# Order of work in a two-layer kernel: attention front, PV sums, norms and kernel spectrum rearranged

## The chip, the cores and the metric

One NeuronCore of a Trainium2 chip runs the whole program. The metric is the device time of one execution in microseconds (us); three executions of the kernel before are given, and one more was profiled. TensorE is called PE, VectorE DVE, ScalarE ACT, GpSimd POOL and SyncE SP, as in the profile.

## The reference, cut to what matters

Four residual steps on x of 2048 positions by 512 channels: attention A, convolution B, A, B, with the same weights both times.

```python
def _A_ref(x, wqkv, wo):          # 32 heads of 16; each position sees 8 positions, 2 apart
    off = jnp.arange(8) * 2
    idx = pos[:, None] - off[None, :]
    ...
    logits = einsum("bhsd,bhswd->bhsw", q, kg) * scale
    logits = where(idx >= 0, logits, -1e9)
    o = einsum("bhsw,bhswd->bhsd", softmax(logits), vg)
    return o.reshape(B, S, D) @ wo

def _B_ref(u, A_re, ..., log_dt, Dskip):
    P = exp(logdA[:, :, None] * l)                # l = 0 .. 2047
    K = einsum("dn,dnl,dn->dl", Cc, P, dB).real   # a kernel of 2048 taps per channel
    y = irfft(rfft(pad(u)) * rfft(pad(K)))[:L]
    return y + u * Dskip

x = A_x
x = x + _A_ref(_layernorm(x), ...)
x = x + _B_ref(_layernorm(x), ...)
x = x + _A_ref(_layernorm(x), ...)
x = x + _B_ref(_layernorm(x), ...)
```

K depends on no x, so its spectrum is made once and used by both B layers.

## The kernel before, in words

Position s = 16 p + a lies on partition p in row a, so `x_sb` is [128, 16, 512] in f32. The source is plain Python that unrolls; a scheduler below it orders each engine's instructions by readiness and source order, and places all semaphores. Pools that are closed hand their memory to pools opened later.

1. `k_gen` makes K: 12 squarings give powers of the state matrix (setup), then four chunks of 32 channel groups build tables `A_r`, `A_i` on DVE (`cmul`, lines 618 to 633), multiply them with `B_r`, `B_n` on PE (line 760) and copy the result to `kgs` on ACT (line 764). Between the chunks `build_b_consts` is stepped: it makes the transform matrices, the large one going to DRAM (`w2_dram`, line 406). At the end 24 transfers write `kgs` to DRAM (line 780).
2. `k_spectrum` reads K back in another order (`k_load`, lines 787 and 803), permutes it to `k_perm` (line 585) and runs the two forward transform steps on it: `f1` (line 486) and `f2` (line 496), in two groups of channels g. The spectrum goes to `kf_dram` (line 599).
3. x is loaded, copied to f32 (line 863), and row sums and sums of squares are taken on ACT (lines 89 and 90).
4. `layer_a`, its front: `ln_finish` makes 1/std of all 16 rows with one power on POOL (line 112), `ln_apply` normalizes, PE transposes to `xnT` (line 148), and k is projected to `kT_ext` (lines 155 to 161). Fourteen rows stand ahead of `kT_ext`, shifted by one partition (lines 164 and 165).
5. `layer_a`, its core, in four quarters q of four rows: q projection (`qproj`); `prod` multiplies q with shifted k on DVE (line 204, 8 a quarter) and PE sums over a head's channels into L (line 207); softmax (lines 213 to 242); `pav` multiplies the weights with shifted v on DVE (line 255, 8 a quarter, one for each shift w and all four rows); PE adds these products up in `po` with the product as the loaded weights and the identity as the moving operand, which also transposes (line 259); `out_proj` (line 275) and the residual (line 95). Products of quarter q + 1 stand between the `pav` of quarter q. The weight for v and the output weight are loaded by `load_a_weights` ahead of the layer.
6. `b_layer`: the norm of all rows to `u`, then `f1`, `f2`; the product with the spectrum read from DRAM in four transfers a tile (lines 527, 528, 531, 532); back with `i1` (lines 543, 544) and `i2` (lines 556, 557) and the residual. `zip_run` runs two steps side by side, always one group's step beside the other's.
7. Layers 4 to 6 again; the last residuals are copied to bf16 on ACT and stored (lines 879, 880).

Of the kernel before, what the change touches and what calls it, by code (L numbers as in the profile page):

```python
# [10 lines left out]
ACT = mybir.ActivationFunctionType  # L11
# [22 lines left out]
POOL_PRODS = ()  # L34
POOL_PAVS = ()
# [7 lines left out]
def build_a_consts(tc, nc, cpool, tpool):  # L43
# [5 lines left out]
    c["ident"] = ident  # L49
# [9 lines left out]
    rows = cpool.tile([1, 2, 512], BF16, name="rows")  # L59
    nc.vector.memset(rows[:], 0.0)  # L60
    nc.vector.memset(rows[:, 0, 0:1], 1.0)
    c["e0"] = rows[:, 0, 0:P]
    c["zrow"] = rows[:, 1, :]
# [8 lines left out]
def load_a_weights(tc, nc, wpool, tmp, A_wqkv, A_wo):  # L72
    wqk = wpool.tile([P, NDT, 2 * D], BF16, name="wqk")
    wsrc = A_wqkv.rearrange("(dt p) c -> p dt c", p=P)
    nc.sync.dma_start(wqk[:], wsrc[:, :, 0:2 * D])
    wvraw = tmp.tile([P, NDT, D], BF16, name="wvraw")
    nc.sync.dma_start(wvraw[:], wsrc[:, :, 2 * D:3 * D])
    wv = wpool.tile([P, NDT, DH, H], BF16, name="wvp")
    nc.scalar.copy(wv[:], wvraw[:].rearrange("p t (h d) -> p t d h", h=H))
    wo = wpool.tile([P, NDT, D], BF16, name="wop")  # L80
    wo_v = A_wo.rearrange("(h q r) c -> r h q c", h=H, q=4, r=4)
    for r in range(4):
        nc.sync.dma_start(wo[r * 32:(r + 1) * 32, :, :], wo_v[r])
    return wqk, wv, wo


def ln_stats_part(nc, lnst, x_sb, a0, a1):
    for a in range(a0, a1):
        nc.scalar.activation(lnst["junk"][:], x_sb[:, a, :], ACT.Identity, accum_out=lnst["s1"][:, a, 0:1])
        nc.scalar.activation(lnst["junk"][:], x_sb[:, a, :], ACT.Square, accum_out=lnst["s2"][:, a:a + 1])  # L90
    nc.vector.memset(lnst["s1"][:, a0:a1, 1:2], 0.0)


def residual_add(nc, lnst, x_row, y_psum, a, part=0):
    nc.vector.scalar_tensor_tensor(x_row, y_psum, 1.0, x_row, ALU.mult, ALU.add, accum_out=lnst["s1"][:, a, part:part + 1])  # L95


def row_sumsq(nc, lnst, x_sb, a):
    nc.scalar.activation(lnst["junk"][:], x_sb[:, a, :], ACT.Square, accum_out=lnst["s2"][:, a:a + 1])  # L99


def ln_finish(nc, pool, lnst):
    mean = pool.tile([P, NA], F32, name="ln_mean")
    nc.vector.tensor_tensor(mean[:], lnst["s1"][:, :, 0], lnst["s1"][:, :, 1], ALU.add)
    nc.vector.tensor_scalar(mean[:], mean[:], 1.0 / D, None, ALU.mult)
    msq = pool.tile([P, NA], F32, name="ln_msq")
    nc.vector.tensor_tensor(msq[:], mean[:], mean[:], ALU.mult)
    veps = pool.tile([P, NA], F32, name="ln_veps")
    nc.vector.scalar_tensor_tensor(veps[:], lnst["s2"][:], 1.0 / D, msq[:], ALU.mult, ALU.subtract)
    nc.vector.tensor_scalar(veps[:], veps[:], EPS, None, ALU.add)  # L110
    rstd = pool.tile([P, NA], F32, name="ln_rstd")
    nc.gpsimd.tensor_tensor(rstd[:], veps[:], lnst["mh"][:], ALU.pow)
    nb = pool.tile([P, NA], F32, name="ln_nb")
    nc.vector.scalar_tensor_tensor(nb[:], mean[:], -1.0, rstd[:], ALU.mult, ALU.mult)
    return rstd, nb
# [9 lines left out]
def layer_a(tc, nc, x_sb, consts, wqk, wv, wo, lnst):  # L125
    ident, ind8 = consts["ident"], consts["ind8"]
    e0, zrow, maskrow = consts["e0"], consts["zrow"], consts["maskrow"]
    scale = float(DH) ** -0.5
    with ExitStack() as ctx:
        big = ctx.enter_context(tc.tile_pool(name="a_big", bufs=1))  # L130
        kT = big.tile([P, NDT, NA + 14, P], BF16, name="kT_ext")
        v = big.tile([P, NA + 14, D], BF16, name="v_ext")
        xnT = big.tile([P, NDT, NA * P], BF16, name="xnT")
        with ExitStack() as c1:
            p1 = c1.enter_context(tc.tile_pool(name="a_p1", bufs=1))
            ps_tr = c1.enter_context(tc.tile_pool(name="a_ps_tr", bufs=2, space=PSUM))
            ps_pj = c1.enter_context(tc.tile_pool(name="a_ps_pj", bufs=4, space=PSUM))
            rstd, nb = ln_finish(nc, p1, lnst)
            nc.vector.memset(lnst["s1"][:, :, 1:2], 0.0)
            xn = p1.tile([P, NA, D], BF16, name="xn")  # L140
            for a in range(NA):
                ln_apply(nc, xn[:, a, :], x_sb[:, a, :], rstd, nb, a, "act" if a % 3 != 2 else "dve")
            for ag in range(2):
                for dt in range(NDT):
                    pt = ps_tr.tile([P, 8, P], BF16, name="pt")
                    for j in range(8):
                        a = ag * 8 + j
                        nc.tensor.transpose(pt[:, j, :], xn[:, a, dt * P:(dt + 1) * P], ident[:])  # L148
                    nc.vector.tensor_copy(xnT[:, dt, ag * 8 * P:(ag + 1) * 8 * P], pt[:].rearrange("p j q -> p (j q)"))
# [17 lines left out]
        with ExitStack() as c2:  # L167
# [134 lines left out]
            for q in range(4):  # L302
# [3 lines left out]
                if n1 is not None:  # L306
                    prod(n1, 0); prod(n1, 1)
# [604 lines left out]
```

## Time and profile before

| | us |
|---|---|
| median of three runs | 721.57 |
| lowest, highest | 715.87, 723.58 |
| the profiled execution | 717.98 |
| its span, first to last instruction | 715.9 |
| busy PE, weight load | 381.7, 286.6 |
| busy DVE | 504.4 |
| busy ACT | 351.0 |
| busy POOL | 13.8 |

The mean granted TensorE clock was 0.802 of full speed. Two kinds of views are used below. In the page's slices the span is cut in 40 parts of 17.9 us, one digit each, the busy share in tenths. In the groups by line a row reads: line, engine, operation, output and inputs, shapes, count; then busy us and mean ns of one; then the idle time of the engine just before them and what ended it. In the views in order of time the first two numbers are start and length in us.

### The profile page before, as it was taken

The page shows a single profiled execution, that of the slowest core. Times are in us where ns is not written, and L with a number is a line of the kernel's source. Part 1 is how long each engine was busy: PE and PEld are TensorE (multiplying, and loading weights), DVE is VectorE, ACT ScalarE, POOL GpSimd, SP SyncE. Part 2 cuts the span into 40 slices and gives each one's busy share as a digit, 9 for nine tenths or more (in the row PEclk, how much of TensorE's full clock was granted, in tenths as well). Part 3 has the DMA queues.
Part 4 walks back from the last instruction along what each step waited for, and adds up shares of the span by engine and source line. Part 5 has one row for each costly group of instructions (what it writes and reads, how often), then busy time and mean ns, then how long its engine had stood idle before and what let it go on. Part 6 is the DMA issues. An engine that isn't in the chain of part 4 may idle for free. (4 is left out here: it accounts for less than half of the span.)

```text
span 715.9 us, 12534 instructions
## 1 busy us (share of the span) xinstructions
PE 381.7 (53%) x5166; PEld 286.6 (40%) x5192; DVE 504.4 (70%) x873; ACT 351.0 (49%) x552; POOL 13.8 (2%) x19
## 2 busy tenths in 40 slices
PE   1000222205500499989675744817998886746763
PEld 1000222205400244567454644714446576526652
DVE  7999999304500348899995867635689999858665
ACT  7998831106479644322332754285432531357524
POOL 0000000000000100000001000010000000010000
PEclk9999955556855599988788778767998987979787
DMA  2002110237661000300002766040003000083622
GB/s 52 0 29 88 60 59 1 73 85 233 214 220 38 0 1 2 103 2 1 2 1 100 234 195 181 1 118 1 1 23 82 2 1 2 2 320 116 195 76 118
DMA packets 28134, 54.28 MB, mean 76 GB/s; under 512 B 9347, under 2 KB 13344, under 8 KB 26144
## 3 DMA queue, kind: packets, MB, share of 16 engines
q1 hardware_dynamic: 25774, 50.87, 22.6%
q10 hardware_dynamic: 2304, 2.62, 1.0%
q8 instruction: 40, 0.66, 0.4%
q14 instruction: 16, 0.13, 0.1%
HBM read 38.67 MB, written 11.14 MB: 70 GB/s over the span
## 5 line engine op out<-in xcount | busy, mean ns | idle before, releaser
L259 PE MATMUL po<-ident,pav 128*128 128x128 bf16 x1024 | 77.4, 250 | 9.0 <-DVE pav L255 8.9
L259 PEld LDWEIGHTS <-pav 128*128 128x128 bf16 x1024 | 74.4, 115 | 11.6 <-DVE pav L255 11.4
L255 DVE TENSOR_TENSOR pav<-attn,v_ext 128x2048 bf16<-128x2048 bf16 x64 | 74.7, 1219 | 4.0 <-PE po L259 3.9
L204 DVE TENSOR_TENSOR prod<-qT,kT_ext 128x2048 bf16<-128x2048 bf16 x64 | 75.0, 1214 | 1.6 <-ACT qT L183 1.6
L760 PE MATMUL pk<-B_r,A_r 128*128 128x84 bf16 x128 | 16.5, 251 | 95.6 <-DVE A_r L629 95.6
L543 PE MATMUL pb<-Wp,t 128*128 128x128 bf16 x256 | 37.4, 240 | 32.6 <-DVE t L531 29.3
L760 PEld LDWEIGHTS <-A_r 128*128 128x128 bf16 x128 | 15.0, 130 | 96.2 <-ACT w_qi L398 66.8
L148 PE MATMUL pt<-ident,xn 128*128 128x128 bf16 x128 | 15.8, 278 | 69.4 <-ACT xn L120 67.2
L266 ACT CAST oT<-po 128x1024 bf16<-128x1024 f32 x8 | 8.1, 1012 | 87.3 <-PE po L259 87.3
L530 ACT CAST ub<-pb 128x1024 bf16<-128x1024 f32 x32 | 32.2, 1030 | 21.0 <-DVE t L532 19.7
L148 PEld LDWEIGHTS <-xn 128*128 128x128 bf16 x128 | 11.3, 124 | 74.6 <-ACT xn L120 71.2
L207 PE MATMUL L<-ind,prod 128*128 128x8 bf16 x1024 | 33.8, 167 | 13.2 <-DVE prod L204 13.1
L207 PEld LDWEIGHTS <-prod 128*128 128x128 bf16 x1024 | 31.2, 97 | 23.8 <-DVE prod L204 16.3
L543 PEld LDWEIGHTS <-t 128*128 128x128 bf16 x256 | 27.6, 109 | 30.1 <-DVE t L531 29.9
L99 ACT ACTIVATE ln_junk<-x_sb 128x512 bf16<-128x512 f32 x48 | 30.2, 629 | 15.2 <-DVE x_sb L95 13.9
L544 PE MATMUL pb<-WpJ,t 128*128 128x128 bf16 x256 | 36.0, 240 | 0.3 <-DVE t L532 0.3
L496 PE MATMUL pb<-a1s,w_sb 128*128 128x64 bf16 x768 | 31.0, 197 | 9.0 <-DVE kf_sb L475 3.3
L285 PE MATMUL pq<-wvp,xnT 128*128 128x512 bf16 x122 | 32.0, 391 | 2.0 <-DVE v_ext L290 1.5
L486 PE MATMUL pb<-F1c,u 128*64 128x128 bf16 x256 | 21.0, 251 | 21.6 <-issue 21.3
L275 PE MATMUL pq<-wop,oT 128*128 128x512 bf16 x120 | 28.9, 379 | 6.7 <-ACT oT L266 6.1
L473 ACT CAST z<-pb 128x1024 bf16<-128x1024 f32 x16 | 16.2, 1012 | 32.7 <-PE pb L544 32.5
L496 PEld LDWEIGHTS <-w_sb 128*128 128x128 bf16 x768 | 27.4, 100 | 12.1 <-issue 9.2
(205 smaller groups left out, 998.7 us busy)
## 6 DMA issues: line engine op xcount, KB each, us to landing
w_sb<-w_dram SPq DMA_DIRECT2D x12, 1024.0 KB, 7.7
kr_c<-kf_dram SPq DMA_DIRECT2D x64, 128.0 KB, 2.9
ki_c<-kf_dram SPq DMA_DIRECT2D x64, 128.0 KB, 2.9
kf_dram<-kf_sb SPq DMA_DIRECT2D x16, 256.0 KB, 2.6
v_ext<-v_ext SPq DMA_DIRECT2D x2, 1568.0 KB, 9.1
w_dram<-w_full SPq DMA_DIRECT2D x4, 512.0 KB, 2.6
w_dram<-w_full ACTq DMA_DIRECT2D x4, 512.0 KB
xin<-in_A_x_dram SPq DMA_DIRECT2D x1, 2048.0 KB
```

What stands on the lines that cost most here:

```text
L99: nc.scalar.activation(lnst["junk"][:], x_sb[:, a, :], ACT.Square, accum_out=lnst["s2"][:, a:a + 1])
L204: eng.tensor_tensor(pr[:], qT[:, ft].unsqueeze(1).to_broadcast([P, NW, 4, P]), kap, ALU.mult)
L207: nc.tensor.matmul(L[:, al, w0 + wi, ft * 8:(ft + 1) * 8], lhsT=pr[:, wi, al, :], rhs=ind8[:], start=False, stop=True, skip_group_check=True)
L255: eng.tensor_tensor(pv[:], attn[:, :, w, :].unsqueeze(2).to_broadcast([P, 4, DH, H]), v[:, s0:s0 + 4, :].rearrange("p a (d h) -> p a d h", ...
L259: nc.tensor.matmul(po[:, al, ftp, :], lhsT=pv[:, al].rearrange("p d h -> p (d h)")[:, ftp * P:(ftp + 1) * P], rhs=ident[:], start=False, s ...
L275: nc.tensor.matmul(pw[:], lhsT=oT[:, al, ftp, :], rhs=wo[:, ftp, :], start=(ftp == 0), stop=(ftp == NDT - 1))
L285: nc.tensor.matmul(pp[:], lhsT=xnT[:, dt, a * P:(a + 1) * P], rhs=wv[:, dt].rearrange("p d h -> p (d h)"), start=(dt == 0), stop=(dt == ND ...
L496: nc.tensor.matmul(p2[:, j, :], lhsT=self.w2[:, ec * EC + j, :], rhs=a1s[:, ec * EC + j, :], start=True, stop=True)
L530: nc.scalar.copy(ub[:], p2[:].rearrange("p e q -> p q e"))
L543: nc.tensor.matmul(p3[:, j, :], lhsT=t1[:, dql, :], rhs=wp_r, start=True, stop=False)
L544: nc.tensor.matmul(p3[:, j, :], lhsT=t2[:, dql, :], rhs=wpj_r, start=False, stop=True)
L760: nc.tensor.matmul(o, lhsT=ta[:, ql].rearrange("p i g -> p (i g)"), rhs=tbb[:, c * CH + ql].rearrange("p b g -> p (b g)"), start=(kx == 0) ...
```

## The change

- The front of layer A becomes `front_block`, for four rows at a time, with its own statistics (first layer), norm (`ln_block`, one power on POOL for four columns), transposes, k projection and shifted copies. In the first layer it is called with x in bf16 after the setup of `k_gen` and after each of its first three chunks; in the second, after each tile of the last `i2` of layer B. The evictions in the first layer are all on ACT. `xnT` is kept for the whole kernel; `u` and one `z` lie in its memory.
- x goes to `x_sb` by four casting transfers on POOL's queue.
- `pav` multiplies for one row and four shifts, and PE adds the products up with the identity as the loaded weights, 512 columns at a time, into one bank. The sum is copied by ACT, transposed by PE (four 128 x 128), copied by ACT again and projected, row by row.
- The zero fill of `po` goes. The maximum over the shifts is one reduction on PSUM, and PE subtracts it in L with a negative identity; the exponential reads L itself.
- All evictions of v go to ACT; v's shifted rows are copied in four parts.
- The norm ahead of layer B is made by blocks inside the core (`norm_u`).
- `k_spectrum` goes. K is written to DRAM in two halves, read back while the first core runs, and transformed in the first layer B, its steps zipped with those of u. The spectrum is written so that both halves of a tile stand twice, and read with one transfer a tile.
- In the last layer one DVE addition per tile writes bf16, which is stored at once.
- In `build_b_consts` index sums move from DVE to POOL, and one of four row copies of a table from ACT to DVE. In `k_gen` several temporaries share memory or become bf16.

```diff
+    def front_block(self, b, x_rows, parts, ln_eng, ev_eng, ext):
+        if parts == 0:
+            for a in range(4):
+                nc.scalar.activation(lnst["junk"][:], x_rows[:, a, :], ACT.Identity, accum_out=lnst["s1"][:, b * 4 + a, 0:1])
+                row_sumsq(nc, lnst, x_rows[:, a, :], b * 4 + a)
+        rstd, nb = ln_block(nc, self.fp, lnst, b * 4, b * 4 + 4, parts)
...
+        for dp in range(2):
+            pt = self.ps_tr.tile([P, 2, 4, P], BF16, name="pt")
...
+            dst = self.xnT[:, 2 * dp:2 * dp + 2, b * 512:(b + 1) * 512]
+            (nc.scalar.copy if ev_eng[dp] == "act" else nc.vector.tensor_copy)(dst, pt[:].rearrange("p t a q -> p t (a q)"))
...
+        (nc.scalar.copy if ext == "act" else nc.vector.tensor_copy)(
+            self.kT[:, :, e0:e1, 1:P], self.kT[:, :, e0 + 16:e1 + 16, 0:P - 1])
...
+                nc.vector.tensor_reduce(mx[:], L[:].rearrange("p a w h -> p a h w"), AX.X, ALU.max)
+                for j in range(2):
+                    nc.tensor.matmul(L[:, 2 * j:2 * j + 2], lhsT=nident[:],
+                                     rhs=mx[:, 2 * j:2 * j + 2].unsqueeze(2).to_broadcast([P, 2, W, H]),
+                                     start=False, stop=True, skip_group_check=True)
+                nc.scalar.activation(ex[:], L[:], ACT.Exp, scale=scale)
...
+                    for wi in range(NW):
+                        w = wg * NW + wi
+                        nc.tensor.matmul(po[:], lhsT=ident[:], rhs=pv[:, wi].rearrange("p d h -> p (d h)"),
+                                         start=(w == 0), stop=(w == W - 1))
+                o = wk.tile([P, 512], BF16, name="o_sb")
+                nc.scalar.copy(o[:], po[:])
...
+                for al in range(4):
+                    pav(q, al)
+                    if al > 0:
+                        out_proj(q, al - 1)
+                    if al == 1 and n2 is not None:
                         qproj(n2)
+                    if n1 is not None:
+                        prod(n1, 4 + al)
+                out_proj(q, 3)
+                for qq in ((), (0, 1), (2,), (3,))[q]:
+                    norm_u(qq)
...
+    def k_f2(self, g):
+            for ri in range(2):
+                self.nc.sync.dma_start(self.kf_dram[g, ec, :, :, ri].rearrange("u p q e -> p u q e"),
+                                       kf[ri * 64:(ri + 1) * 64].unsqueeze(1).to_broadcast([64, 2, DQG, EC]))
...
+    for q in range(4):
+        nc.gpsimd.dma_start(x_sb[:, q * 4:(q + 1) * 4, :], x_v[:, q * 4:(q + 1) * 4, :])
...
+    k_load(tc, nc, kr, kd)
+    la.core(x_sb, u)
...
+    zip_run(fb.f1(0, kp, "ka"))
+    zip_run(fb.f1(1, kp, "ka"), fb.k_f2(0), lead=2)
+    zip_run(fb.f1(0, u, "ua"), fb.k_f2(1), lead=2)
+    zip_run(fb.f1(1, u, "ua"), fb.u_f2(0), lead=2)
+    zip_run(fb.u_f2(1), fb.i1(0), lead=2)
...
+    zip_run(fb.i1(1), fb.i2(0, None), lead=2)
...
+    zip_run(fb.i2(1, lambda t: la.front_block(t, x_sb[:, t * 4:(t + 1) * 4, :], 2, ["act", "dve", "act", "dve"],
+                                              ["act", "dve", "act", "dve", "act", "dve"], "dve")))
...
+    la.core(x_sb, u)
```

More of the change, by code (lines that the diff above doesn't have):

```diff
@@ L98, in row_sumsq, with residual_add @@
[L98 to L114, printed above, removed]
+def residual_add(nc, lnst, x_row, y_psum, x_in, a, part=0):
+    nc.vector.scalar_tensor_tensor(x_row, y_psum, 1.0, x_in, ALU.mult, ALU.add, accum_out=lnst["s1"][:, a, part:part + 1])
```

678 lines of the change are left out of this document (336 added, 342 removed).

## The prediction

> **What bounds the kernel now.** I read the page's slices first (where DVE and ACT are idle), then busy time by stage, then the groups by line for prices, then the order on DVE, PE and SP at the seams.
>
> ```profile
> DVE  7999999304500348899995867635689999858665
> ACT  7998831106479644322332754285432531357524
> ```
>
> ```profile
> 0.00:61.50 61.50, 3.53 (x24) 2.14 (x24) 56.46 (x129) 54.89 (x105) 1.53 (x13) 1.00 0.11 32
> 61.50:137.00 75.50, 16.79 (x256) 15.53 (x256) 67.75 (x131) 35.47 (x58) 0.00 (x0) 0.73 0.11 42
> 137.00:167.50 30.50, 0.00 (x0) 0.00 (x0) 0.41 (x1) 0.00 (x0) 0.00 (x0) 0.52 0.59 143
> 167.50:204.50 37.00, 19.69 (x512) 17.83 (x512) 20.02 (x17) 21.75 (x19) 0.00 (x0) 0.78 0.67 247
> 204.50:268.70 64.20, 24.24 (x138) 13.16 (x142) 15.13 (x30) 47.95 (x90) 3.25 (x2) 0.64 0.11 30
> 268.70:398.50 129.80, 101.15 (x1219) 69.83 (x1228) 114.22 (x158) 45.17 (x80) 2.91 (x1) 0.85 0.13 45
> 398.50:463.50 65.00, 43.47 (x806) 40.28 (x807) 45.10 (x80) 31.31 (x32) 0.00 (x0) 0.79 0.48 137
> 463.50:509.00 45.50, 25.57 (x158) 14.85 (x159) 19.78 (x60) 28.88 (x52) 3.25 (x2) 0.75 0.16 47
> 509.00:640.40 131.40, 101.86 (x1226) 71.02 (x1235) 115.25 (x159) 46.85 (x83) 2.90 (x1) 0.87 0.15 51
> 640.40:715.90 75.50, 45.42 (x832) 42.01 (x832) 50.30 (x112) 38.71 (x36) 0.00 (x0) 0.82 0.44 134
> ```
>
> The columns are stretch, length, then busy time of PE, weight load, DVE, ACT, POOL, then granted clock, DMA share, GB/s. In order the rows are: kernel generation (two rows); its round trip through DRAM, with every engine idle; the kernel spectrum; x, statistics and layer A's front; attention core 0 with the norm behind it; layer B's transforms up to the last one; that last one with the second front; core 1 with its norm; the second layer B. DVE fills generation (124.2 of 137.0) and the cores (114.2 of 129.8). The 131.7 us from 137.0 to 268.7 hold 35.6 us of DVE work and 69.7 of ACT: waits in a row. That is where a change of order can gain.
>
> **1. The front beside generation.** Prices:
>
> ```profile
> L89 ACT ACTIVATE ln_junk<-x_sb 128x512 bf16<-128x512 f32 x16 | 10.1, 629 | 0.4
> L89 ACT ACTIVATION_READ_ACCUMULATOR ln_junk<-x_sb 128x1 f32 x16 | 3.0, 186 | 0.0
> L530 ACT CAST ub<-pb 128x1024 bf16<-128x1024 f32 x32 | 32.2, 1030 | 21.0 <-DVE t L532 19.7 <-PE pb L496 1.3
> L159 ACT CAST kT_ext<-pp 128x512 bf16<-128x512 f32 x16 | 9.4, 585 | 20.2 <-PE pp L155 20.2
> L164 ACT COPY kT_ext<-kT_ext 128x3556 bf16<-128x3556 bf16 x2 | 6.3, 3156 | 2.1 <-DVE kT_ext L161 2.1
> L405 ACT ACTIVATE w_full<-w_sc,dmask_k 128x512 bf16<-128x512 f32 x32 | 20.6, 710 | 0.6 <-DMA w_dram<-w_full 0.5
> L120 ACT ACTIVATE xn<-x_sb,ln_nb,ln_rstd 128x512 bf16<-128x512 f32 x22 | 15.7, 800 | 7.4 <-DVE ln_nb L114 7.4
> L122 DVE TENSOR_SCALAR xn<-x_sb,ln_rstd,ln_nb 128x512 bf16<-128x512 f32 x10 | 4.7, 542 | 0.1
> L109 DVE SCALAR_TENSOR_TENSOR ln_veps<-ln_s,ln_msq 128x16 f32<-128x16 f32 x4 | 0.7, 176 | 10.8 <-ACT ln_junk L99 10.6 <-ACT ln_junk L90 0.2
> L112 POOL TENSOR_TENSOR ln_rstd<-ln_veps,ln_mh 128x16 f32<-128x16 f32 x4 | 11.6, 2903 | 321.4 <-DVE ln_veps L110 171.7 <-ACT ln_junk L99 147.5 <-DMA v_ext<-rows 2.2
> ```
>
> ACT gets 32 statistics passes x 0.815 = 26.1, 8 transposed evictions x 1.03 = 8.2, 16 kT evictions x 0.585 = 9.4 and the shifted copy of kT, both halves, 2 x 3.156 = 6.3; it loses 8 x 0.71 = 5.7. That is +44.3 on 90.4: 134.7. Its idle time in the second row (75.5 - 35.5 = 40.0) takes nearly all of it. DVE gets 16 norm applications and 8 table rows at no more than 0.542 each (13.0) and 20 small operations x 0.176 = 3.5: at most +16.5. Ten table sums leave it for POOL; for these I take off 3.5: +13. POOL's table sums and the matmuls (64 transposes, 64 projections) lie on engines that the first two rows show idle. Each block's shift waits for its power, and the table products queue behind it on DVE, the matmuls that make the kernel behind those. So DVE 124.2 + 13 + its 12.8 idle = 150; I add 1 us for each of the four rstd powers (POOL, 0 to 2.9 each; a block has 4 columns in place of 16) and 2 for the first q projection: the first product at **156** in place of 268.7. Bounds: 145 (additions all in idle time) and 175 (half of ACT's 44.3 does not fit). If the cover were gone, the 44.3 would be paid in full. The x load for this moves from late in SP's queue to its front, and the f32 copy of x to POOL's queue; the first use of it is the first residual, over 20 us into the core.
>
> By the Trainium skill, page VectorE: DVE Perf Modes, section The perf-mode tier table (the rule you actually need), a bf16 scalar operation between SBUF tensors runs four times as fast as the plain rate; which the row does not reach on f32 input; by its figures I estimate 0.30 us for 512 elements where the row has 0.542, 24 of them 5.8 us less: 150 for the first product by the page, 156 by the row. No run so far shows this operation on bf16 input.
>
> **2. Round trip under the core.** 30.5 us of idle time go; what can come late instead is the weight for v, which layer A's `load_wv_wo` issues on SP behind the kernel rows:
>
> ```profile
> 136.41 0.35 SPq L458 DMA_DIRECT2D w_sb<-w_dram  x1
> 136.80 14.83 SPq L780 DMA_DIRECT2D kd_dram<-kgs  x24
> 152.15 9.04 SPq L803 DMA_DIRECT2D k_rl<-kd_dram  x17
> ```
>
> Only half of the kernel rows (24 issues, now smaller) are still to be written then, but with the reads some 24 us of issues stand ahead of it if SP keeps source order. DVE has 16 products (16 x 1.2 = 19) and two softmaxes to do meanwhile. Between 0 and +24 I take +6: SP issued a `w_sb` load, which stands behind these writes in the source, ahead of them, so it does not keep source order.
>
> **3. The core.**
>
> ```profile
> L204 DVE TENSOR_TENSOR prod<-qT,kT_ext 128x2048 bf16<-128x2048 bf16 x64 | 75.0, 1214 | 1.6 <-ACT qT L183 1.6
> L255 DVE TENSOR_TENSOR pav<-attn,v_ext 128x2048 bf16<-128x2048 bf16 x64 | 74.7, 1219 | 4.0 <-PE po L259 3.9
> L225 DVE TENSOR_TENSOR Ls<-Ls,mx 128x1024 f32<-128x1024 f32 x8 | 9.7, 1218 | 0.1
> L220 DVE TENSOR_TENSOR m<-Ls 128x512 f32<-128x512 f32 x8 | 5.5, 688 | 1.7 <-ACT Ls L214 1.7
> L290 DVE CAST v_ext<-pq 128x512 bf16<-128x512 f32 x16 | 10.8, 686 | 4.5 <-PE pq L285 4.5
> L475 DVE CAST kf_sb<-pb 128x1024 bf16<-128x1024 f32 x11 | 13.1, 1218 | 14.0 <-DMA kf_dram<-kf_sb 12.2 <-PE pb L496 1.8
> L95 DVE SCALAR_TENSOR_TENSOR x_sb<-pq,x_sb 128x512 f32<-128x512 f32 x32 | 21.3, 683 | 9.1 <-PE pq L275 9.1
> ```
>
> ```profile
> 286.64 2.75 PE L285 MATMUL pq<-wvp,xnT 128*128 128x512 bf16 x12 [0.47 <-DVE v_ext L290]
> 297.12 0.94 PE L259 MATMUL po<-ident,pav 128*128 128x128 bf16 x14
> ```
>
> ```profile
> 294.28 11.44 DVE L204 TENSOR_TENSOR prod<-qT,kT_ext 128x2048 bf16<-128x2048 bf16 x10 [0.79 <-ACT qT L183]
> 627.06 0.69 DVE L95 SCALAR_TENSOR_TENSOR x_sb<-pq,x_sb 128x512 f32<-128x512 f32 x1 [3.30 <-PE pq L275]
> ```
>
> DVE's 32 products and 32 attention-times-v multiplications keep count and size, 77.9 us a layer: this floor does not move. The stationary identity is neutral on PE: 512 matmuls of 128 columns at 0.94/14 = 0.067 are 34, 128 of 512 columns at 2.75/12 = 0.23 are 29; 64 transposes x 0.067 = 4.3 take the difference. Softmax loses the subtraction and the largest maximum pass for one reduction (priced as an eviction of the same 1024 elements, `kf_sb`): 4 x (1.218 + 0.688 - 1.218) = -2.7. v's evictions leave DVE, 8 x 0.686 = -5.5 (ACT takes them; it is at 45 of 130). Of these 8.2 I count half, -4. The norm behind the core ran on 16 rows at once: 16.6 us from the last multiplication (627.06 less its 3.30 of wait) to the first transform at 640.40. By blocks only four rows are left there: 3.3 us of wait, 0.7 residual, five small operations 0.9, one power, two applications on ACT 1.6: 10 to 11, so -6. Against that, a row's sum now goes PE, ACT copy, PE transpose, ACT copy, PE projection, DVE. Before, residuals waited 9.1 us for 32 rows; I allow 0.3 more a row, +5, and +3 for three powers inside the core. 129.8 - 4 - 6 + 5 + 3 = 128, with part 2 **133**; core 1 **128**.
>
> **4. Layer B.**
>
> ```profile
> 407.60:429.00 21.40, 11.84 (x272) 10.58 (x271) 14.62 (x21) 12.97 (x14) 0.00 (x0) 0.76 0.57 166
> 429.00:452.00 23.00, 13.05 (x206) 12.07 (x204) 14.27 (x19) 9.36 (x10) 0.00 (x0) 0.78 0.50 146
> 423.24 1.18 SPq L527 DMA_DIRECT2D kr_c<-kf_dram  x2
> L879 ACT CAST xo<-x_sb 128x2048 bf16<-128x2048 f32 x4 | 7.3, 1894 | 4.5 <-DVE x_sb L95 4.5
> ```
>
> The two stages that read the spectrum take 44.4 us with DVE busy 28.9: four issues a tile at 0.59 are 2.4 us, for 16 tiles 38. One issue a tile of the same bytes leaves DVE as the limit: 15 us a stage. The spectrum moves in (37.0 before): a first transform alone (9, as from 398.5 to 407.6), one stage beside its second half and one beside the first transform of u, 16 evictions each (8 x 1.22 on DVE = 9.8). Both halves of a tile are now written twice; DVE's evictions waited 12.2 us for such writes before, so I take 15 here too, not 10. Sum: 2 (permutation) + 9 + 4 x 15 + 11.5 (from 452.0 to 463.5) = **82**. Of the second layer's 75.5 these stages leave 10.5 for the end; it swaps 7.3 us of ACT copies for four additions of 1.22 on DVE beside the matmuls, 9: 9 + 15 + 15 + 11.5 + 9 = **60**.
>
> **5. Second front inside the last transform.** Per block ACT 4 x 0.815 + 2 x 0.80 + 1.03 + 2 x 0.585 = 7.1, DVE 6.5 in the same way. Four blocks 28, and 10 to fill and to empty: **38** for 45.5.
>
> Sum: 156 + 133 + 82 + 38 + 128 + 60 = 597. The profiled execution takes 717.98, 2.1 over its span: 599. The runs' median, 721.57, is 0.5% above it: **602**.
>
> **Rivals.** (a) ACT becomes generation's bound and half its additions are exposed: +22, 624. For: 134.7 of 150 is 90%, and statistics stand ahead of the chains. Against: 40 us idle.
> (b) Slower: DVE stands still for each row's residual in the new chain. Price: 8 wide matmuls 1.8, 4 transposes 0.3, one copy 0.6, hand-overs about 0.8: 3.5 a row; at half clock 5.4; taken as 4.5, 32 rows cost 144: 746. It ends above 721.57 from 3.7 us a row. Against: the ten products in a row above are not in the source's order, so other work is put into such gaps; for: in each layer's last quarter there are no products to put there.
> (c) POOL holds DVE up: 16 powers in place of 4, each exposed at 2.9, are 35 us more, of which about 8 are in the sum: 629. Against: a quarter of the columns. By the Trainium skill, page SBUF — State Buffer, section SBUF: two separate sides, POOL and a DVE operation with two SBUF inputs exclude each other for a whole instruction, and loads from POOL's queue can starve; every power before met an idle DVE, so no run here shows it.
> (d) The doubled spectrum writes bound their stages: 16 evictions at twice the former 37 - 9 = 28 us are 56 in place of 30: 628.
> (e) It does nothing because DVE's work hardly falls: excluded but for (b), since the 131.7 us that go are mostly waits.
>
> **Chances.** Forecast 0.63 (own range 583 to 618), (a) 0.14, (b) 0.05, (c) 0.07, (d) 0.07; better than 583, 0.04. The range 575 to 640 leaves out about 0.1. A change under 1% can't be told from none here: faster 0.94, same 0.02, slower 0.04, all of the last from (b).
>
> **What would show it.** First product at 148 to 163; no stretch with all engines idle; DVE over 85% in the cores; one spectrum load a tile and stages near 15 us; last residual to first transform under 11 us. Wrong: DVE idle before residuals of over 1 us a row, ACT full past 150 us, or the first attention-times-v multiplication over 35 us behind the first product.

## The result and the profile after

The changed kernel takes **639.19 us**, median of four runs (636.87 to 643.93), beside 719.30 (715.87 to 723.58) for the kernel before in the same runs: a ratio of 0.889, 95% interval 0.882 to 0.897. The profiled execution took 638.53 us with a span of 636.8. The forecast was 602. The time lies at the upper end of the stated range of 575 to 640, and 21 us above the forecast's own range of 583 to 618; it is also longer than each of the rivals (a), (c) and (d) was priced at (624 to 629).

The page of the kernel after, DVE and ACT by slices of 15.9 us:

```profile
DVE  3889999985464999884555678856688979848776
ACT  3999888976640354346645362496514243348631
```

No slice is empty any more, but in the cores DVE is more often at 4 to 8 than at 9. The kernel after by stages; the columns are those of the same table before (stretch, length, busy PE, weight load, DVE, ACT, POOL, clock, DMA share, GB/s):

```profile
0.00:156.40 156.40, 47.02 (x418) 31.61 (x419) 128.95 (x294) 128.08 (x253) 16.61 (x29) 0.83 0.18 57
156.40:298.90 142.50, 99.24 (x903) 49.58 (x901) 105.69 (x151) 61.90 (x111) 10.89 (x9) 0.85 0.29 66
298.90:348.70 49.80, 35.74 (x816) 32.53 (x816) 27.88 (x24) 28.21 (x28) 0.00 (x0) 0.78 0.75 244
348.70:398.30 49.60, 31.40 (x504) 29.24 (x498) 35.43 (x74) 21.79 (x22) 0.36 (x1) 0.79 0.61 202
398.30:442.60 44.30, 32.75 (x195) 16.82 (x196) 28.70 (x82) 31.72 (x60) 10.04 (x5) 0.88 0.11 25
442.60:572.10 129.50, 97.87 (x879) 48.38 (x877) 104.19 (x148) 52.36 (x101) 4.93 (x4) 0.83 0.15 51
572.10:636.80 64.70, 46.24 (x832) 43.14 (x832) 48.15 (x56) 31.14 (x32) 0.00 (x0) 0.84 0.45 156
```

In order: generation with the first front, up to the first product; core 0 with its norm; layer B while the spectrum is written; the rest of layer B up to the last residual of i2(0), the last transform step of the first channel group; i2(1), the same step of the second group, with the second front; core 1; the second layer B. Against the stages before, the first product comes 112.3 us earlier (268.7 to 156.4), and the second layer B is 10.8 us shorter; core 0 is 12.7 longer and the first layer B, which now makes the spectrum, 34.4 longer (65.0 to 99.4). Beside the terms of the forecast:

| term | forecast | measured | off |
|---|---|---|---|
| first product | 156 | 156.4 | +0.4 |
| core 0 | 133 | 142.5 | +9.5 |
| layer B up to i2(0) | 82 | 99.4 | +17.4 |
| i2(1) and second front | 38 | 44.3 | +6.3 |
| core 1 | 128 | 129.5 | +1.5 |
| second layer B | 60 | 64.7 | +4.7 |
| sum | 597 | 636.8 | +39.8 |

Five rows from the list of DVE's waits in the kernel after (what waited, for what, us in total, times, longest):

```profile
DVE prod L223 <- ACT qT L203: 17.8, 5, 6.2
DVE x_sb L72 <- PE pq L284: 15.9, 14, 1.8
DVE t L543 <- DMA kf_c<-kf_dram: 11.9, 13, 3.2
DVE kf_sb L499 <- DMA kf_dram<-kf_sb: 11.0, 7, 5.4
DVE pav L264 <- DMA v_ext<-v_ext: 5.6, 1, 5.6
```

Of the first row 6.2 us lie ahead of the first product. Three of the five are for transfers; in layer B, where two of these stand, the forecast had DVE as the limit. One more loss is in no list of waits, since it hides in durations. The timeline of DVE and of POOL in the second front:

```profile
405.40 0.16 DVE L96 TENSOR_TENSOR ln_nb<-ln_nm,ln_rstd 128x4 f32<-128x4 f32 x1 [0.71 <-POOL ln_rstd L94]
405.48 5.93 DVE L85 TENSOR_SCALAR ln_nm<-ln_nm 128x4 f32<-128x4 f32 x1
405.55 5.86 DVE L72 SCALAR_TENSOR_TENSOR x_sb<-pb,x_sb 128x256 f32<-128x256 f32 x1
412.04 0.15 DVE L89 SCALAR_TENSOR_TENSOR ln_msq<-ln_nm 128x4 f32<-128x4 f32 x1
```

```profile
405.31 6.06 POOL L308 MEMSET v_ext<- 1x7168 bf16 x1
```

An operation on four columns, 0.17 us in other blocks, takes 5.93: it ends with POOL's memset of v's zero row (405.31 + 6.06 = 411.37), and all of DVE stands behind it. Before, a DMA brought that row.

### The profile page after: what moved, and what is told of

It is laid out like the page before. It is cut to its first block, busy times and chain, and to the rows that moved or that the text cites. A ratio compares the mean times of both kernels' runs of the same rounds, so it can differ in the third digit from the quotient of the medians.

```text
span 636.8 us, 11210 instructions
## 1 busy us (share of the span) xinstructions
PE 390.3 (61%) x4536; PEld 251.3 (39%) x4536; DVE 479.0 (75%) x825; ACT 355.2 (56%) x605; POOL 42.8 (7%) x47
## 4 chain that ended last, share of the span: by engine, by line
DVE 34%; PE 31%; ACT 14%; DMA 10%; issue 5%; POOL 3%; SPq 1%; DVEq 0%; POOLq 0%; ACTq 0%
PE po L268 8%; DMA kf_c<-kf_dram 5%; DVE prod L223 4%; PE pq L299 4%; PE pb L510 3%; DVE x_sb L72 3%; PE pq L284 3%; DVE pav L264 3%; POOL ln_rstd L94 3%; PE pq L201 2%; DVE t L543 2%; ACT ln_junk L76 2%; DVE t L544 2%; DVE cm_a L612 2%; DVE cm_b L613 1%
## 5 line engine op out<-in xcount | busy, mean ns | idle before, releaser
L268 PE MATMUL po<-pav,ident 128*128 128x512 bf16 x256 | 76.8, 441 | 21.2 <-DVE pav L264 21.1
L271 ACT CAST o_sb<-po 128x512 bf16<-128x512 f32 x32 | 18.7, 584 | 74.2 <-PE po L268 74.2
L268 PEld LDWEIGHTS <-ident 128*128 128x128 bf16 x256 | 27.2, 109 | 59.0 <-issue 42.2
L519 PE MATMUL pb<-a1s,w_sb 128*128 128x64 bf16 x768 | 35.0, 206 | 20.0 <-ACT ub L542 6.7
L148 PE MATMUL pt<-ident,xn 128*128 128x128 bf16 x128 | 13.2, 256 | 51.7 <-DVE xn L104 49.6
L94 POOL TENSOR_TENSOR ln_rstd<-ln_veps,ln_mh 128x4 f32<-128x4 f32 x16 | 21.1, 1320 | 340.5 <-DVE ln_veps L92 317.9
L499 ACT CAST a1s<-pb 128x1024 bf16<-128x1024 f32 x30 | 30.1, 1016 | 24.4 <-PE pb L510 24.0
L284 PE MATMUL pq<-wop,oT 128*128 128x512 bf16 x128 | 34.0, 389 | 10.5 <-ACT oT L281 10.1
L154 PE MATMUL pp<-xnT,wqk 128*128 128x512 bf16 x128 | 32.9, 398 | 7.4 <-ACT xnT L150 4.2
L72 DVE SCALAR_TENSOR_TENSOR x_sb<-pq,x_sb 128x512 f32<-128x512 f32 x32 | 22.0, 687 | 15.9 <-PE pq L284 15.9
L543 DVE TENSOR_TENSOR t<-ub,kf_c 128x1024 bf16<-128x1024 bf16 x32 | 22.1, 690 | 14.4 <-DMA kf_c<-kf_dram 11.9
```

Source lines behind the costliest of these rows:

```text
L72: nc.vector.scalar_tensor_tensor(x_row, y_psum, 1.0, x_in, ALU.mult, ALU.add, accum_out=lnst["s1"][:, a, part:part + 1])
L94: nc.gpsimd.tensor_tensor(rstd[:], veps[:], lnst["mh"][:, 0:n], ALU.pow)
L268: nc.tensor.matmul(po[:], lhsT=ident[:], rhs=pv[:, wi].rearrange("p d h -> p (d h)"), start=(w == 0), stop=(w == W - 1))
L284: nc.tensor.matmul(pw[:], lhsT=oT[:, ftp, :], rhs=wo[:, ftp, :], start=(ftp == 0), stop=(ftp == NDT - 1))
L519: nc.tensor.matmul(p2[:, j, :], lhsT=self.w2[:, ec * EC + j, :], rhs=a1s[:, ec * EC + j, :], start=True, stop=True)
L543: nc.vector.tensor_tensor(t1[:, :, ec * EC:(ec + 1) * EC], ub[:], kc[:, 0], ALU.mult)
```

## Experiments

Stages are compared in single profiled executions, times by ratios to the kernel before in the same runs (the changed kernel: 0.889, 0.882 to 0.897).

**The zero row in pieces**

```diff
-            nc.gpsimd.memset(v[0:1, 0:14, :], 0.0)
+            for s14 in range(14):
+                nc.gpsimd.memset(v[0:1, s14:s14 + 1, :], 0.0)
```

> The zero row of the extended v (one POOL memset of 1x7168, 6.06 us in the changed kernel) is written in 14 memsets of 1x512 instead. Theory (POOL holds up the one-operand DVE operations for as long as one POOL instruction lasts): the 5.9 us stall of DVE in the second front goes, each remaining stall is at most one piece of about 0.45 us, and the stretch from the last residual of the first half of layer B to the first product of core 1 falls from 44.3 us to 38 to 40; the time falls by 4 to 6 us. Rival (the second front is bound by its chain ACT, POOL, DVE, PE, and the stall only takes the place of waits): that stretch falls by less than 1 us. Second rival (the wait is for something else than POOL): the stall of 5.9 us stays where it is.

629.41 us, ratio 0.875 (0.872 to 0.879); i2(1) with the second front 40.1 us. The same place in this kernel:

```profile
403.01 0.37 DVE L85 TENSOR_SCALAR ln_nm<-ln_nm 128x4 f32<-128x4 f32 x1
403.43 1.44 DVE L104 TENSOR_SCALAR xn<-x_sb,ln_rstd,ln_nb 128x512 bf16<-128x512 f32 x2
```

The stall is gone, though POOL writes as long as before (14 pieces, 6.59 us in core 0): DVE's operation now takes 0.37 us, about one piece. The first theory holds, and is worth about 4 us. The total fell by 10; the rest lies in core 1 (126.0, at a clock of 0.87 there in place of 0.83), core 0 (140.8) and layer B (98.1), and is not shown to come from the edit.

**The spectrum written once, read with a repeated row**

```diff
-                self.nc.sync.dma_start(self.kf_dram[g, ec, :, :, ri].rearrange("u p q e -> p u q e"),
-                                       kf[ri * 64:(ri + 1) * 64].unsqueeze(1).to_broadcast([64, 2, DQG, EC]))
+                self.nc.sync.dma_start(self.kf_dram[g, ec, 0, :, ri], kf[ri * 64:(ri + 1) * 64])
...
+            src = bass.AP(tensor=half.tensor, offset=half.offset, ap=[[0, 2], [2 * DQG * EC, 64], [1, 2 * DQG * EC]])
```

> Each tile of the kernel spectrum is written to DRAM once instead of twice (32 issues of 128 KB in place of 256 KB) and read by one issue that takes the same 64 rows for both halves of the partitions. Theory (the bytes written bound the spectrum stages): the 39.9 us in which SP issues the 32 writes fall to 20 to 30, first layer B 99.4 us to 85 to 90, second layer B stays at 64.7 within 2. Rival (the number of issues bounds them, about 1.25 us each): first layer B stays within 2 us of 99.4. Second rival (two readers of the same DRAM rows are slower): second layer B over 67.

866.29 us, ratio 1.202 (1.200 to 1.205): layer B up to i2(0) takes 218 us, the second layer B 174. The DMA view of this kernel from 400 to 480 us, all such reads: share of the 16 engines in tenths, GB/s, issues:

```profile
DMA  1111111111111111111111111111111111111111
GB/s 53 53 49 53 53 53 53 53 53 53 49 53 53 53 49 53 53 53 49 53 53 53 49 53 53 53 53 57 53 53 53 49 53 53 53 49 53 53 53 49
kf_c<-kf_dram SPq DMA_DIRECT2D x8, 512.0 KB
```

An issue whose outermost dimension is the repetition, 2, moves 53 GB/s on about a tenth of the engines, and that hides everything behind the first read. The writes come before it, from 64 partitions as in the changed kernel, and can be compared. Their 32 issues took 30.5 us in place of 39.9, but the clock of that stretch was 0.91 in place of 0.78. The run with the zero row in pieces, which writes everything twice, had 0.89 there. Its stretch from the first transform to the first read, and the same of this run:

```profile
296.76:344.61 47.85, 32.51 (x816) 29.48 (x816) 27.89 (x24) 27.94 (x28) 0.00 (x0) 0.89 0.79 254
297.81:338.07 40.26, 30.95 (x790) 27.90 (x791) 26.45 (x24) 26.97 (x27) 0.00 (x0) 0.91 0.69 205
```

At nearly the same clock the 32 writes take 30.5 us in place of 38.1. So writing half of the bytes is worth about 7.6 us here: the first theory has the mechanism, and just misses its 20 to 30 us. The clock is worth less: over the runs that leave these writes alone the stretch goes from 47.9 us (at 0.89) to 52.4 (at 0.74). DVE still waited 8.8 us for the writes (11.0 in the changed kernel).

**Written once from 128 partitions, read by two issues**

```diff
+            self.nc.sync.dma_start(self.kf_dram[g, ec, 0].rearrange("p i q e -> i p q e"), kf[:])
...
+            for u in range(2):
+                nc.sync.dma_start(kc[u * 64:(u + 1) * 64], self.kf_dram[g, ec, 0])
```

> Each tile of the kernel spectrum is written to DRAM once, by one issue from all 128 partitions (16 issues of 256 KB in place of 32), and read by two plain issues, one for each half of the partitions, from the same rows; no row is repeated inside an issue. Theory (bytes and issues of the doubled writes bound the spectrum stages, which wait for the DMA to free their buffers): the wait of the evictions for the writes goes, first layer B 99 us to 84 to 90, second layer B 64.7 to 66 at most. Rival (the writes are hidden behind the transforms on TensorE and the reads are the bound): first layer B over 95. Second rival (two readers of the same rows are slow, as in the run with the repeated row): second layer B over 80.

696.16 us, ratio 0.968 (0.965 to 0.971): layer B up to i2(0) 148 us, the second layer B 71.7. The write fell into the same trap: its destination has 2 as the outermost dimension. The DMA view of this kernel from 330 to 350 us:

```profile
DMA  1111112111111111111111111111955111111111
GB/s 45 53 49 49 53 53 82 49 53 53 53 45 53 49 49 49 57 49 49 49 57 49 49 49 53 53 49 49 193 209 213 49 53 53 49 49 53 53 49 49
```

In the second layer B nothing is written and no row repeated: its +7 us is the price of two reads of 64 partitions, of the same rows, in place of one read of 128. So the doubled writes of the changed kernel, which cost some 7.6 us once, save some 7 us of reading here, and likely as much in the first layer, which this run can't show.

**Half of the spectrum read**

```diff
-            nc.sync.dma_start(kc[:], self.kf_dram[g, ec].rearrange("u p i q e -> (u p) i q e"))
+            nc.sync.dma_start(kc[:, 0], self.kf_dram[g, ec, :, :, 0].rearrange("u p q e -> (u p) q e"))
```

> Only the real half of each tile of the kernel spectrum is read (256 KB in place of 512 KB an issue) and used for both products; the imaginary half is left out of the computation. Theory (the reads bound the two stages of each layer B that multiply by the spectrum, at about 280 GB/s, 1.9 us a tile): first layer B 99 us to 86 to 92, second 64.7 to 57 to 61. Rival (the products and evictions on VectorE and TensorE are the bound, and DMA only looks full): both within 2 us.

625.74 us, ratio 0.872 (0.869 to 0.875). The second layer B falls from 64.7 to 59.1, as the theory has it; the first only from 99 to 95, against 86 to 92. Its stretch from the first read to the last residual of i2(0):

```profile
348.35:392.75 44.40, 31.79 (x512) 29.82 (x512) 35.52 (x74) 22.02 (x23) 0.35 (x1) 0.77 0.45 131
```

That is 5.2 us less than the 49.6 of the changed kernel (48.6 to 51.1 in the runs that leave layer B alone); the stretch with the writes was 1.2 us longer here, at a clock of 0.72. DVE's wait for the reads goes from 11.9 to 5.9 us. So the reads are one bound of these stages, worth about 5 us in each layer, and not the larger part of the first layer's excess.

**The kernel rows read later**

```diff
-    k_load(tc, nc, kr, kd)
-    la.core(x_sb, u)
+    la.core(x_sb, u, lambda: k_load(tc, nc, kr, kd))
...
+            if after_v is not None:
+                after_v()
```

> The reads of the kernel rows from DRAM are issued in the source behind the projections for v instead of ahead of the loads of the weights for v and the output. Theory (core 0 is late by the shifted copy of v, which stands behind these reads on SP's queue, and by the load and permutation of the weight for v that holds up q): only the first part goes, the 5.6 us of wait before the first attention-times-v multiplication; core 0 falls from 142.5 us to 136 to 138. Rival (all of the 13 us over core 1 are SP's order): 130 to 132. Second rival (the reads are then late for layer B): core 0 shorter, but a new wait of the first transform, time unchanged.

643.56 us, ratio 0.893 (0.890 to 0.896); core 0 148.0 us: a miss. The copies of v are now issued first, from 172 us on, but land late. DMA share by slices and two of the issues of this kernel from 170 to 200 us (KB each, median us to landing), and the first attention-times-v multiplications:

```profile
DMA  1569799999999999999999999999998623014122
x_sb<-in_A_x_dram POOLq DMA_DIRECT2D x4, 1024.0 KB, 12.0
v_ext<-v_ext SPq DMA_DIRECT2D x3, 448.0 KB, 19.2
```

```profile
197.32 4.63 DVE L264 TENSOR_TENSOR pav<-attn,v_ext 128x2048 bf16<-128x2048 bf16 x4 [6.25 <-DMA k_rl<-kd_dram]
```

The copy takes 19.2 us (6.4 in core 0 of the changed kernel, where it goes last), beside the f32 load of x on POOL's queue, while the DMA engines are full. The multiplications still wait 6.25 us for a transfer, but begin 41.9 us behind the first product in place of 49.5: the order on SP's queue does matter to them. Core 0 is longer all the same. DVE's order is another one here, and its waits for residuals in core 0 are 10.2 us in place of 6.0; why is not isolated.

**x loaded behind v**

```diff
+            nc.gpsimd.tensor_copy(x_sb[96:97, q * 4, 0:1], v[96:97, 13, 0:1])
             nc.gpsimd.dma_start(x_sb[:, q * 4:(q + 1) * 4, :], x_v[:, q * 4:(q + 1) * 4, :])
```

> The load of x in f32 on POOL's queue starts only when the shifted copy of v has landed (one element of each part of x is written from it first); order of the other transfers as in the changed kernel. Theory (that load fills the DMA engines from 172 to 206 us and so makes the shifted copy of v late): the first attention-times-v multiplication comes before 198 us in place of 205.9, core 0 142.5 us to 135 to 139. Rival (the copy of v is late because it stands behind the reads of the kernel rows on SP's queue): first multiplication at 203 to 206, core 0 unchanged or longer. Second rival (the multiplication is early, but x comes late for the first residuals, or TensorE is the next bound): core 0 within 2 us of 142.5.

631.86 us, ratio 0.880 (0.876 to 0.884). Core 0 of this kernel; then what SP issued and the first attention-times-v multiplications, in the changed kernel and in this one:

```profile
155.50:293.20 137.70, 100.55 (x903) 50.13 (x901) 105.60 (x151) 61.88 (x110) 11.42 (x13) 0.84 0.26 68
```

```profile
171.31 18.12 SPq L787 DMA_DIRECT2D k_rl<-kd_dram  x17
192.64 0.59 SPq L305 DMA_DIRECT2D v_ext<-v_ext  x1
205.90 4.63 DVE L264 TENSOR_TENSOR pav<-attn,v_ext 128x2048 bf16<-128x2048 bf16 x4 [5.59 <-DMA v_ext<-v_ext]
```

```profile
169.26 9.87 SPq L789 DMA_DIRECT2D k_rl<-kd_dram  x17
181.91 0.59 SPq L305 DMA_DIRECT2D v_ext<-v_ext  x1
198.71 0.69 DVE L253 TENSOR_TENSOR attn<-ex,rs 128x1024 bf16<-128x1024 bf16 x1
199.32 4.62 DVE L264 TENSOR_TENSOR pav<-attn,v_ext 128x2048 bf16<-128x2048 bf16 x4
```

They follow the softmax without a wait, at 199.32 in place of 205.90 (1.3 later than the expectation's bound), and core 0 is 4.8 us shorter, within it. Half of the 9.5 us was the load of x. The way is not the one expected, though: a copy of v takes as long to land as before (6.5 us, 6.4 in the changed kernel). What the load of x slowed is the issuing of the reads of the kernel rows, 18.12 us in place of 9.87 (15.5 to 18.4 in the runs with the early load that keep this order, 9.6 to 9.9 in the three with the late one), and the copies of v, which stand behind them on SP's queue, were issued some 11 us later for it. Load and queue act together.

**Norms at the end; the front's place in the source**

```diff
-                for qq in ((), (0, 1), (2,), (3,))[q]:
+                for qq in ((), (), (), (0, 1, 2, 3))[q]:
```

> The norms by blocks of four rows, which the changed kernel finishes as rows come, are all put behind the last row of each core. Theory (finishing early takes about 6 us off the end of each core): core 0 142.5 to 148 to 150 and core 1 129.5 to 135 to 137, the time 11 to 15 us longer. Rival (three early blocks cost as much inside the core, where DVE is busy, as they save behind it): within 3 us of the changed kernel.

640.85 us, ratio 0.890 (0.887 to 0.892); core 0 142.7, core 1 129.7. The front was moved in the source, too: its four blocks are called behind all of generation.

```diff
-        if c < 3:
-            front0(c + 1)
...
+    for b in range(4):
+        front0(b)
```

> The four blocks of the first attention front run behind the end of kernel generation instead of beside it; all else as in the changed kernel. Theory (beside generation the front costs what it adds to DVE and to its waits, some 18 us, and behind it its own chain of about 45 us): first product at 180 to 190 us in place of 156.4, the time 24 to 34 us longer. Rival (generation already waits for ACT, so that taking the front out of it gives back nearly all): first product at 156 to 165.

634.18 us, ratio 0.882 (0.878 to 0.887); first product at 161.7, core 0 133.7. Neither says what it was made for. In the first kernel a norm still runs between the last residuals, in the second the front's statistics run 40 us ahead of the end of generation (timelines of the two):

```profile
284.65 0.55 DVE L104 TENSOR_SCALAR xnT<-x_sb,ln_rstd,ln_nb 128x512 bf16<-128x512 f32 x1
285.11 0.68 DVE L72 SCALAR_TENSOR_TENSOR x_sb<-pq,x_sb 128x512 f32<-128x512 f32 x1
```

```profile
104.12 0.61 ACT L76 ACTIVATE ln_junk<-xin 128x512 bf16<-128x512 bf16 x1
```

Here instructions do not stand in the order of the source, so a dependency is needed to hold work back. The second kernel does show that the front's place is not settled: its first product comes 5.2 us later, and its core 0 still ends 3.6 us earlier (at 295.3).

**The front really held**

```diff
+    def front0(b, kgs):
+        nc.vector.tensor_copy(lnst["junk"][0:1, 0:1], kgs[0:1, 0, P // 2 - 1:P // 2])
...
+        if c == 3:
+            b_steps(100)
+            for b in range(4):
+                front0(b, kgs)
```

> The first front is really kept behind kernel generation: its statistics wait for one element of the last evicted chunk of the kernel (in the run that only moved the front's place in the source, the first block still ran from about 60 us on, since instructions are not issued in the order of the source). Loads of x stay early. Theory (the front beside generation is worth most of its own chain): generation alone ends at 135 to 142 us, four blocks of about 12 us of ScalarE each follow, first product at 182 to 196, core 0 some 5 to 9 us shorter since the projections for v no longer come late, the time 20 to 32 us longer than the changed kernel. Rival (generation waits for ScalarE so much that the front only changes places with it): first product at 156 to 168, the time within 8 us.

670.30 us, ratio 0.934 (0.930 to 0.938), 31 us above the changed kernel. This kernel by stages:

```profile
0.00:144.80 144.80, 22.92 (x280) 20.20 (x280) 122.37 (x258) 86.01 (x160) 7.52 (x25) 0.89 0.16 53
144.80:208.30 63.50, 39.84 (x204) 18.55 (x209) 9.20 (x40) 55.28 (x111) 11.79 (x9) 0.84 0.51 134
208.30:329.10 120.80, 84.74 (x823) 43.27 (x833) 104.82 (x151) 48.57 (x93) 6.76 (x4) 0.81 0.08 18
```

The theory holds in the time; its parts were larger. The first product comes at 208.3, 52 us later (182 to 196 expected), since ACT is busy for 55.28 of the 63.50 us; core 0 is 22 us shorter (5 to 9 expected), since 13 of the 16 rows of v are projected when it starts. Its first attention-times-v multiplications:

```profile
232.79 4.62 DVE L264 TENSOR_TENSOR pav<-attn,v_ext 128x2048 bf16<-128x2048 bf16 x4
```

They come without a wait, 24.5 us behind the first product; in the changed kernel it is 49.5 in core 0 and 24.7 in core 1. Up to the end of core 0 the front beside generation is worth 329.1 - 298.9 = 30 us. And with v nearly ready a core 0 takes 120.8: in the changed kernel its head, up to these multiplications, is bound by the projections and the copy of v, not by DVE.

**The sums with moving identity, row by row**

```diff
-                        nc.tensor.matmul(po[:], lhsT=ident[:], rhs=pv[:, wi].rearrange("p d h -> p (d h)"),
-                                         start=(w == 0), stop=(w == W - 1))
+                        for ftp in range(NDT):
+                            nc.tensor.matmul(po[:, ftp, :], lhsT=pv[:, wi].rearrange("p d h -> p (d h)")[:, ftp * P:(ftp + 1) * P],
+                                             rhs=ident[:], start=False, stop=True, skip_group_check=True)
```

> The sums over the window in attention-times-v go back to the form of the kernel before (products as weights, the identity moving, 128 columns at a time, started by a product with a zero row), still one row of tokens at a time; the copy of the sum and its four transposes fall away, since the sum comes out transposed. Theory (neutral on TensorE, and the shorter chain of a row gives back a part of the 9.9 us that DVE waits for residuals in core 1): core 1 129.5 us to 123 to 129, the time 0 to 12 us shorter. Rival (four times as many instructions and weight loads make TensorE the bound of a row): DVE waits for the sums in PSUM, core 1 over 135.

632.47 us, ratio 0.878 (0.873 to 0.884). The sums in the kernel after, and in this one, and core 1 in this one:

```profile
L268 PE MATMUL po<-pav,ident 128*128 128x512 bf16 x256 | 76.8, 441 | 21.2 <-DVE pav L264 21.1
```

```profile
L270 PE MATMUL po<-ident,pav 128*128 128x128 bf16 x1024 | 77.0, 246 | 22.1 <-DVE pav L266 22.1
```

```profile
442.70:566.10 123.40, 96.00 (x1217) 67.42 (x1217) 104.34 (x148) 44.73 (x85) 4.94 (x4) 0.83 0.14 46
```

Neutral on TensorE: 76.8 beside 77.0 us. But core 1 falls from 129.5 to 123.4 with the same DVE work: without the copy and the transposes a row's chain is shorter. DVE's waits there for residuals go from 9.9 to 7.8 us, and for the exponentials from 3.2 to 0.5. So the stationary identity, with the copy and the transposes that it asks for, costs some 6 us a core where the core is not held up by v; core 0, which is, keeps 141.4.

**Edits together.** First the pieces, the moving identity and the late x.

> Three edits together on the changed kernel: the zero row of v in 14 pieces, the sums of attention-times-v with moving identity, the f32 load of x behind the shifted copy of v. Theory (they act at different places: second front, residual chains, head of core 0): the sum of their parts, 4 + 8 + 7, some 19 us less than the changed kernel, 616 to 624 us. Rival (the residual chain and the late copy of v cover the same idle time of core 0): 10 to 14 us less, 625 to 630.

620.11 us, ratio 0.865 (0.861 to 0.869): the first theory. Core 0 137.0, i2(1) with the second front 39.8, core 1 122.5. Then a version with the DMA for the zero row in place of the pieces, the weight for v permuted on DVE, and an earlier second q projection:

```diff
-        nc.scalar.copy(self.wv[:], wvraw[:].rearrange("p t (h d) -> p t d h", h=H))
+        nc.vector.tensor_copy(self.wv[:], wvraw[:].rearrange("p t (h d) -> p t d h", h=H))
...
+            nc.sync.dma_start(v[0:1, 0:14, :], self.c["zrow"].unsqueeze(1).to_broadcast([1, 14, D]))
...
+                if i == 5:
+                    qproj(1)
```

> As the run with three edits, with the zero row of v brought by a DMA from a row of zeros (as the kernel before did) in place of the POOL pieces, the permuting copy of the weight for v on DVE instead of ScalarE, and the second q projection ahead of the last four projections for v. Theory (in the head of core 0 DVE waits 16 us for q because ScalarE first copies the weight, 3.9 us, and TensorE first ends the projections for v): first products no longer wait 3.5 us, those of the second part wait under 1.5 us in place of 3.7; core 0 137 to 128 to 134, second front 40.1 to 38 to 40, the time 4 to 10 us less than with three edits, 610 to 616. Rival (what is won at the head is lost again at the shifted copy of v, whose DMA is then what comes last): core 0 within 2 us of 137, 618 to 622.

622.22 us, ratio 0.864 (0.862 to 0.867): no difference from three edits that these intervals can tell, where 4 to 10 us were expected. Core 0 is 134.0 and the second front 36.9, as expected or better, but core 1 is 124.5, and the medians agree. Both kernels are faster than the changed kernel, and than the one before.

## Why the prediction was right and where it was not

- **First product, 156: the mechanism was right, the exact hit is luck.** The front's work on ACT fits beside generation: 128.08 of 156.4 us busy, no bound. The kernel's last eviction comes about 10 us later with the front (154.6) than without (144.8). But two terms missed by the same amount in opposite directions. DVE's work rose by 4.7 us (124.2 to 128.95) where 13 were added, and DVE stood idle for 27.5 us where 12.8 + 4 + 2 were counted. The norm's application was priced at 0.542 us, from f32 input; on bf16 input it took 0.404, which is also above the estimate of 0.30. Of the idle time, 6.2 us are for the first q, 3.3 for powers and some 8 for ACT at the start. There a small case of rival (a) shows: the first statistics wait 5.96 us for x, and ACT's work for the kernel stands behind them. The norm's group, rows of DVE's waits up to the first product, and ACT's first statistic:

```profile
L104 DVE TENSOR_SCALAR xn<-xin,ln_rstd,ln_nb 128x512 bf16<-128x512 bf16 x16 | 5.7, 404 | 0.0
```

```profile
DVE prod L223 <- ACT qT L203: 6.2, 1, 6.2
DVE t L682 <- ACT in_C_re L653: 4.3, 1, 4.3
DVE in_A_re L651 <- ACT dt_bf L640: 3.5, 1, 3.5
DVE ln_nb L96 <- POOL ln_rstd L94: 3.3, 4, 0.9
```

```profile
12.08 0.63 ACT L138 ACTIVATE ln_junk<-xin 128x512 bf16<-128x512 bf16 x1 [5.96 <-DMA xin<-in_A_x_dram]
```
- **Round trip and v, "+6": the place was right, the size and the cause not.** The weight for v did not come late: its load was issued at 153.92, ahead of the writes. What came late behind the reads on SP's queue is the shifted copy of v. The step that failed stands in part 1: the f32 load of x was put at nothing because its first use is 20 us into the core. It is 4.8 of the 9.5 us, since it slows the issuing of the reads ahead of that copy. The rest is not isolated. Inside core 0 DVE waits another 8.1 us for q: 3.5 behind ACT's copy of the weight for v, 3.7 behind v's projections. The last run, which moves both among other edits, took core 0 from 137.0 to 134.0. The sign named for this, the first attention-times-v multiplication over 35 us behind the first product, came: 205.9 - 156.4 = 49.5.
- **Layer B, 82: the step that failed is "one issue a tile of the same bytes leaves DVE as the limit: 15 us a stage".** The stretch with the writes takes 49.8 where 2 + 9 + 15 + 15 = 41 were counted, the stretch with the reads 49.6 where it was 41.5. Of the 8.8 us over in the first, the doubled bytes written are about 7.6 by the run that wrote half (30.5 against 38.1 us at nearly the same clock); the clock of 0.78 can be the rest. Of the 8.1 us over in the second, the reads are 5.2 by the run with half of them; 2.9 stay open. DVE, the limit by the forecast, is busy for 27.88 of 49.8 us and 35.43 of 49.6. Rival (d), the doubled writes, had a mechanism that took place, at under a third of its price of 26.
- **Second front, 38: the term lacked an operation.** The diff turns the DMA of v's zero row into a POOL memset; the forecast did not price it. Rival (c) had the mechanism, on the powers: these cost 1.32 us each and 13.4 us of waits in all, the memset held DVE for 5.9 at once. The Trainium skill, page SBUF — State Buffer, section SBUF: two separate sides, has both halves of this: POOL shuts out a one-operand DVE operation that uses two ports, for a whole instruction, but a POOL operation that only writes leaves products of two SBUF tensors alone. The trace agrees: the operation of 0.17 us took 5.93 beside the memset of core 1, and two products ran at 156.43 in 2.36 us, full speed, while the memset of core 0 ran (153.96 to 160.02).
- **Core 1, 128: right by its sum, not by its terms.** DVE's work is 104.2, but it is busy for 80% and not 85 (74% in core 0). The row chain was priced at +5; the waits for residuals grew by 5.4 (4.5 to 9.9), and with the moving identity the core is 6.1 us shorter. 0.5 us a row is far from rival (b)'s 3.7.
- **Norms by blocks: borne out, not isolated.** From the start of the last multiplication (560.02) plus its 1.22 us to the first transform (572.14) it is 10.9 us, against 16.6 before and 10 to 11 forecast; the run made to undo it did not.
- **Second layer B, 60: its stages were read as DVE's.** 4.7 over; with half of the reads it is 59.1.
- **The gain itself.** The run that holds the front behind generation shows 30 us of it. That the round trip and the spectrum no longer stand alone (30.5 and 37.0 us before) was not undone by a run; the stages show it, and also that the spectrum's new place costs the first layer B 34.4 us. The total came out 37 us over the forecast since every term missed to the same side, the largest by transfers where DVE had been taken as the limit.

## What to carry to other kernels

When a stage's stall is removed, price the transfers that remain in bytes as well as in issues, and list every load that the change lets start at the same time: a transfer with a late first use can still delay an earlier one, and it can do so by holding up the queue that issues it. Look at when a transfer is issued before blaming its flight. Look for operations that change engine as a side effect of an edit, down to a memset, and ask which engine they shut out. To undo a part in an experiment, hold it by a dependency and see in the trace that it moved.

## What was not expected of the hardware

A DMA whose outermost dimension is 2, on either side, ran at 49 to 53 GB/s, on reads with a repeated row and on writes without one; issues with 64 or 128 outermost reached 210 (32 writes of 256 KB in 39.9 us) and 280 (16 reads of 512 KB in 29.9 us). The Trainium skill, page DMA: Bandwidth & Descriptors, section Rules for kernel authors, has this rule: an outermost dimension of less than 16 confines a DMA to at most as many engines. The trace agrees: the reads with outermost 2 used 12.8% of the time of 16 engines, which is that of two. SP took 18.12 us to issue 17 reads while a load of 4 x 1 MB was under way on POOL's queue, and 9.87 without it. And a memset of one partition by POOL is slow: 6.06 us for 7168 elements, no less in 14 pieces.
